# Chunked attention with a top-2 router: V read in its natural rows and spread to chunk contexts by selection matmuls

## The chip, the cores and the metric

The kernel runs on one core of a Trainium2 chip. The metric is the device time of one execution in microseconds (us). Engines are called by their names in the profile: PE (matmuls; its weight loads are PEld), DVE (vector), ACT (scalar), POOL (GpSimd), and SP, which only issues transfers. Each runs its instructions in order. DMAs are issued from the queues of POOL, SP and ACT. PSUM, into which PE writes, has eight banks here: three go round under the tag "tr" and five under the tag "w".

## The reference

Two parts follow one another. Attention over chunks of 32 positions: a chunk sees 16 positions to its left, 8 to its right, and 8 memory rows, so 64 keys in all, fewer at the two ends of a sequence. Then a mixture of experts in which each token goes to its two best of eight.

```python
B, H, S, D = q.shape                      # 4, 8, 768, 64; mem_k, mem_v: 8 rows per head
chunk, left_ctx, right_ctx = (32, 16, 8)
for c in range(S // chunk):
    c_start, c_end = c * chunk, c * chunk + chunk
    l_start, r_end = max(0, c_start - left_ctx), min(S, c_end + right_ctx)
    k_full = np.concatenate([mem_k, k[:, :, l_start:r_end]], axis=2)
    v_full = np.concatenate([mem_v, v[:, :, l_start:r_end]], axis=2)
    scores = scale * np.matmul(q[:, :, c_start:c_end], k_full.transpose(0, 1, 3, 2))
    a = softmax(scores)
    out[:, :, c_start:c_end] = np.matmul(a, v_full)
...
x = out.transpose(0, 2, 1, 3).reshape(B * S, H * D)          # 3072 tokens of 512
noisy = x @ w_gate + np.log1p(np.exp(x @ w_noise)) * noise   # 8 experts
# the two best experts of each token, softmax of their two logits as weights
out[token] += weight * (np.maximum(x[token] @ w1[e], 0) @ w2[e])
```

## The kernel before

**Pairs and groups.** Attention works on 16 pairs: batch b, and the heads hp and hp + 4 (hh = 0 and 1), which lie on partitions 0 to 63 and 64 to 127 wherever the head dimension or a context is on the partitions. Two pairs of one batch make a group; `load_group` (L290) loads Q, K and V of one group into one of three sets of buffers (tiles qn, kn, vf), and every load of Q, K and V is issued from POOL's queue. Q and K come in natural rows: position t * 128 + p of a head is on partition p, so all 128 partitions are written.

**V before.** V comes already cut into contexts (L300 to L319): the tile vf has 64 partitions for each head, 56 for the window of a chunk and 8 for the memory rows, and 24 chunks along the free dimension. The windows overlap (56 rows for every 32), so V is read 1.75 times. The memory rows are loaded once for every chunk (a broadcast of 24) by four DMAs per group, issued from SP's queue. SP's queue also carries the fill of the router's table with blank rows (`fill_blank`, L87, 3.7 MB). The first window of a sequence reaches before its start and the last beyond its end; there vf holds rows of a neighbouring head, or zeros at the ends of the whole tensor. `cast_v` (L322) turns one pair's vf into the bf16 tile vwin: one ACT copy for the 22 inner chunks, and two DVE multiplications for the edge chunks with a column `live` of zeros and ones, which sets padded rows to zero. A 65th column of vwin holds ones (the same `live` in edge chunks), so that the last matmul gives the softmax's sum with its numerator.

**The stages of a pair.** `qkT` (L369): twelve fp32 transposes of Q and K on PE into "tr" banks, four ACT copies to bf16. `scores` (L390): for each of 24 chunks and two heads one matmul of 32 queries with 56 keys (in edge chunks two pieces, padded keys being scored with real ones that V's zeros drop later, `context`, L382) and one with the 8 memory keys, into two "w" banks; then maximum and subtraction on DVE and the exponent on ACT. `probT` (L417): six transposes of the probabilities on PE and a DVE copy. `mix` (L433): 48 matmuls of probabilities with vwin into two "w" banks, then reciprocal and product on DVE into the row of the token.

**The order.** The loop at L453 runs the stages of four pairs against each other: `qkT(n)`, `scores(n-1)`, `probT(n-2)`, `cast_v(n-2)`, `mix(n-3)`. A planner turns this into one order per engine, in which neighbouring pairs can be interleaved. After the last pair of a batch its router work (`dispatch`, L128) is queued as a list of small steps, and each call of `tick()` between the stages takes one step of it; what is left runs after the loop. It ends in indirect stores to the table x_by_pair from POOL's queue. Then the experts follow (from L473), which the change does not touch.

Of the kernel before, what the change touches and what calls it, by code (L numbers as in the profile page):

```python
# [12 lines left out]
F32 = mybir.dt.float32  # L13
# [8 lines left out]
def kernel(  # L22
# [267 lines left out]
    def load_group(b, g, fine=False):  # L290
        qn = apool.tile([128, HV, BT, 2, D], F32, name="qn", bufs=3)
        kn = apool.tile([128, HV, BT, 2, D], F32, name="kn", bufs=3)
        step = 1 if fine else HV
        for i in range(0, HV, step):
            for dst, src in ((qn, q), (kn, k)):
# [4 lines left out]
        vf = apool.tile([128, HV, ncnk, D], F32, name="vf", bufs=3)  # L300
        for hh in range(2):
            p0 = 64 * hh
            h0 = HP * hh + HV * g
            o0 = v[b, h0, 0].offset - left_ctx * D
            dst = vf[p0:p0 + WIN].rearrange("p h c d -> p (h c) d")
            src = lambda c, n, j=0, nj=WIN: bass.AP(v.tensor, o0 + (c * chunk + j) * D, [[D, nj], [chunk * D, n], [1, D]])
            nch = HV * ncnk
            lo, hi = 0, nch
            if b == 0 and h0 == 0:
                nc.vector.memset(vf[0:32, 0, 0, :], 0.0)  # L310
                nc.gpsimd.dma_start(out=dst[left_ctx:, 0:1, :], in_=src(0, 1, left_ctx, WIN - left_ctx))
                lo = 1
            if b == B - 1 and h0 + HV == H:
                nc.vector.memset(vf[p0 + 32:p0 + 64, HV - 1, ncnk - 1, :], 0.0)
                nc.gpsimd.dma_start(out=dst[:WIN - right_ctx, nch - 1:nch, :], in_=src(nch - 1, 1, 0, WIN - right_ctx))
                hi = nch - 1
            nc.gpsimd.dma_start(out=dst[:, lo:hi, :], in_=src(lo, hi - lo))  # L317
            for i in range(HV):
                nc.sync.dma_start(out=vf[p0 + WIN:p0 + CTX, i], in_=mem_v[b, h0 + i].rearrange("m (o d) -> m o d", o=1).to_broadcast([n_mem, ncnk, D]))  # L319
        groups_in[b, g] = (qn, kn, vf)  # L320

    def cast_v(n):  # L322
        b, hp = divmod(n, HP)
        vf = groups_in[b, hp // HV][2]
        vw = vwins[n % len(vwins)]
        nc.scalar.copy(vw[:, 1:ncnk - 1, 0:D], vf[:, hp % HV, 1:ncnk - 1, :])  # L326
        for c, col in ((0, live[:, 0:1]), (ncnk - 1, live[:, 1:2])):
            V.tensor_scalar(out=vw[:, c, 0:D], in0=vf[:, hp % HV, c, :], scalar1=col, scalar2=None, op0=Alu.mult)
# [362 lines left out]
```

## Time and profile before

| what | value |
|---|---|
| runs | 525.01 us median of 3 (519.53, 525.01, 526.74) |
| profiled execution | 515.7 us, span 513.9 us |
| mean granted PE clock over the span | 0.79 of full speed |
| attention | 0 to about 213 us |
| rest of the router, up to the first expert's input | about 213 to 262 us |
| experts | about 262 to 513.9 us |

All rows come from one profiled execution. A row that groups instructions gives line, engine, operation, output and inputs, shapes, count, then busy time and the mean of one in ns, and behind the second bar the idle time of the engine just before them with what ended it ("issue" where the engine waited for nothing that the profile shows). A row of the order of time begins with start and length in us. A row of a window begins with its limits. The slices divide the span into 40 equal parts of 12.85 us, each digit a busy share in tenths. A row of waits names who waited for whom, with total, times and longest in us. DMA rows give the size of one issue in KB and the median time from issue to landing.

### The profile page before, as it was taken

Reading aid. Unit: us, or ns where it says so; the run is one execution under the profiler, and the core shown is the slowest. Engines: PE = TensorE matmul, PEld = TensorE weight load, DVE = VectorE, ACT = ScalarE, POOL = GpSimd, SP = SyncE. Lnnn points to the kernel's source line nnn. Section 1 sums busy time; section 2 is a strip of 40 time slices with the busy share of each in tenths; the row PEclk is TensorE's granted clock in tenths of the full one; section 3 lists DMA queues with packets and bytes.
Section 4 is the critical chain, followed back from the end, with each engine's and each line's share of the span. In section 5 each row is a group of like instructions: output and inputs, shape, how many; then the busy total and the mean of one; then the engine's idle time right before and its main releaser. Section 6 shows DMA issues by size and latency. Waiting matters only on the chain. (4 is left out here: it accounts for less than half of the span.)

```text
span 513.9 us, 10712 instructions
## 1 busy us (share of the span) xinstructions
PE 322.8 (63%) x4561; PEld 198.2 (39%) x4561; DVE 171.3 (33%) x537; ACT 142.9 (28%) x237; POOL 138.5 (27%) x210
## 2 busy tenths in 40 slices
PE   1516243005164677444119969969999999999992
PEld 1415232004153556322005425536454545454540
DVE  1121423003156643955513112123141433333331
ACT  1232330005264356451201322313232213131200
POOL 9543433105050060063331001020211330313132
PEclk9999565557585775655556987989999999999997
DMA  8999999929777440039832453561574865661111
GB/s 118 182 237 236 221 210 212 191 52 117 142 109 149 61 113 13 4 91 202 173 91 71 70 86 74 83 125 29 100 145 82 166 146 85 141 111 67 39 67 64
DMA packets 41843, 60.06 MB, mean 117 GB/s; under 512 B 14171, under 2 KB 29624, under 8 KB 41793
## 3 DMA queue, kind: packets, MB, share of 16 engines
q0 software_dynamic: 23008, 49.93, 50.3%
q1 hardware_dynamic: 18464, 9.35, 9.4%
q8 instruction: 37, 0.61, 0.5%
q10 hardware_dynamic: 320, 0.07, 0.1%
q14 instruction: 14, 0.11, 0.1%
HBM read 62.73 MB, written 14.47 MB: 150 GB/s over the span
## 5 line engine op out<-in xcount | busy, mean ns | idle before, releaser
L559 PE MATMUL ps_h<-xTb,w1t 128*128 128x384 bf16 (+4 forms) x832 | 113.4, 293 | 1.0 <-DVE xTb L501 1.0
L594 PE MATMUL ps_y<-w2t,ht 128*128 128x512 bf16 x448 | 98.0, 379 | 0.0
L559 PEld LDWEIGHTS <-w1t 128*128 128x128 bf16 x832 | 62.0, 99 | 44.8 <-issue 4.6
L563 ACT ACTIVATE ht<-ps_h 128x512 bf16<-128x512 f32 x64 | 38.2, 597 | 122.5 <-PE ps_h L559 97.1
L594 PEld LDWEIGHTS <-ht 128*128 128x128 bf16 x448 | 43.2, 98 | 51.4
L565 DVE TENSOR_SCALAR ht<-ps_h 128x416 bf16<-128x416 f32 x64 | 37.9, 592 | 65.8 <-PE ps_h L559 65.8
L378 PE MATMUL p_t<-ident,kn 128*128 128x128 f32 x96 | 23.1, 392 | 48.9 <-ACT qT L379 41.1
L601 POOL DMA_INDIRECT out_dram<-acc,tid x28 | 27.8, 994 | 78.6 <-DVE acc L600 41.5
L317 POOL DMA_DIRECT2D vf<-in_v_dram x16 | 22.6, 1417 | 80.1 <-ACT kT L379 32.8
L600 DVE SCALAR_TENSOR_TENSOR acc<-ps_y,meta,acc 128x512 f32<-128x512 f32 x28 | 21.0, 751 | 54.5 <-PE ps_y L594 54.5
L254 POOL DMA_INDIRECT x_by_pair<-xrow,slot_i x24 | 23.9, 998 | 50.9 <-issue 33.1
L378 PEld LDWEIGHTS p_t<-ident,kn 128*128 128x128 f32 x96 | 16.8, 204 | 52.0 <-ACT qT L379 43.3
L598 ACT ACTIVATE acc<-ps_y,meta 128x512 f32<-128x512 f32 x28 | 19.2, 687 | 61.3 <-PE ps_y L594 61.3
L407 DVE TENSOR_REDUCE mx<-ps_s 128x6 f32<-128x384 f32 x32 | 16.6, 552 | 54.0 <-PE ps_s L402 50.6
L413 ACT ACTIVATE P<-sd 128x384 bf16<-128x384 f32 x32 | 15.6, 519 | 56.6 <-DVE sd L412 56.6
L326 ACT CAST vwin<-vf 128x1408 bf16<-128x1408 f32 x16 | 21.0, 1359 | 36.2 <-DMA vf<-in_mem_v_dram 33.1
L378 PE MATMUL p_t<-ident,qn 128*128 128x128 f32 x96 | 23.7, 415 | 10.7 <-DMA qn<-in_q_dram 10.7
L402 PE MATMUL ps_s<-mkT,qT 64*32 64x8 bf16 x768 | 18.6, 173 | 17.3 <-issue 17.3
L401 PE MATMUL ps_s<-kT,qT 64*32 64x56 bf16 (+3 forms) x832 | 20.5, 202 | 13.1 <-issue 11.9
L441 PE MATMUL ps_o<-vwin,PT 64*32 64x65 bf16 x768 | 11.8, 219 | 23.8 <-issue 23.8
L402 PEld LDWEIGHTS <-qT 64*32 64x32 bf16 x768 | 15.6, 100 | 19.5 <-issue 19.1
L298 POOL DMA_DIRECT2D qn<-in_q_dram x18 | 18.1, 1006 | 17.6 <-PE p_t L378 10.3
(137 smaller groups left out, 351.7 us busy)
## 6 DMA issues: line engine op xcount, KB each, us to landing
vf<-in_v_dram POOLq DMA_DIRECT2D x14, 672.0 KB, 21.5
w1t<-in_moe_w_dram POOLq DMA_DIRECT2D x8, 1024.0 KB, 8.1
w2t<-in_moe_w_dram POOLq DMA_DIRECT2D x8, 1024.0 KB, 10.1
qn<-in_q_dram POOLq DMA_DIRECT2D x14, 384.0 KB, 19.9
kn<-in_k_dram POOLq DMA_DIRECT2D x14, 384.0 KB, 21.6
x_by_pair<-blank SPq DMA_DIRECT2D x1, 3696.0 KB
xl<-x_by_pair SPq DMA_DIRECT2D x28, 132.0 KB
vf<-in_mem_v_dram SPq DMA_DIRECT2D x32, 48.0 KB
```

Source lines behind the costliest of these rows:

```text
L254: nc.gpsimd.indirect_dma_start(out=xd_tile[t0 + t], out_offset=bass.IndirectOffsetOnAxis(ap=slot_i[:, t:t + 1], axis=0), in_=xrow[:, t, :] ...
L317: nc.gpsimd.dma_start(out=dst[:, lo:hi, :], in_=src(lo, hi - lo))
L326: nc.scalar.copy(vw[:, 1:ncnk - 1, 0:D], vf[:, hp % HV, 1:ncnk - 1, :])
L378: nc.tensor.transpose(out=p_t[:, t * 128:(t + 1) * 128], in_=src[:, hp % HV, g * HT + t, :, :], identity=ident)
L401: nc.tensor.matmul(out=o[:, a:z], lhsT=ql, rhs=kT[hs, t:t + z - a], start=True, stop=True)
L402: nc.tensor.matmul(out=o[:, WIN:], lhsT=ql, rhs=mkT[hs, hp, b * n_mem:(b + 1) * n_mem], start=True, stop=True)
L559: nc.tensor.matmul(out=ps_h[:, off:off + n], lhsT=w1t[:, kp, f * 128:(f + 1) * 128], rhs=rhs(kp), start=(kp == 0 and i == 0), stop=(kp == ...
L563: nc.scalar.activation(out=ht[:, f, lo:hi], in_=ps_h[:, :hi - lo], func=Act.Relu)
L565: nc.vector.tensor_scalar(out=ht[:, f, lo:hi], in0=ps_h[:, :hi - lo], scalar1=0.0, scalar2=None, op0=Alu.max)
L594: nc.tensor.matmul(out=ps_y, lhsT=ht[:, f, j * CAP:(j + 1) * CAP], rhs=w2t[:, f, :], start=(f == 0), stop=(f == FB - 1))
L600: nc.vector.scalar_tensor_tensor(out=acc[p], in0=ps_y, scalar=gate, in1=acc[p], op0=Alu.mult, op1=Alu.add)
L601: nc.gpsimd.indirect_dma_start(out=out_tile[p], out_offset=bass.IndirectOffsetOnAxis(ap=tid[p][:, 0:1], axis=0), in_=acc[p], in_offset=Non ...
```

## The change

V is loaded like Q and K, in natural rows over 128 partitions (tile vn), each row once. DVE casts a pair's V to bf16 (tile vb). PE then builds the contexts: a chunk's window is picked from the 128 rows of its block by a matmul with columns of the identity (`sel`), for all six blocks at once, once for each of the four chunks of a block (rr) and each head. The first chunk of a block takes its left rows from the block before, the last its right rows from the block behind (`sel_x[:, 0]` and `[:, 1]`), added up in the same PSUM tile. The memory rows are loaded once for the whole kernel on ACT's queue (mv_nat, next to mk_nat), and are added by one more matmul (`sel_x[:, 2 + b]` with mvz). Four ACT copies per pair bring the result (ps_v, "w" banks) into vwin. Padded keys are now scored -1e30 times 64 by a matmul of two constant tiles (`one_q`, `far`), so the column of ones needs no `live`, and `live`, `keep` and `context` go. In the loop `cast_v` moves to iteration n, next to `qkT(n)`, with a `tick()` of its own, and `spread(n-1)` stands in two halves before and after `probT(n-2)`.

```diff
@@ -288,72 +288,75 @@
     groups_in = {}
 
     def load_group(b, g, fine=False):
-        qn = apool.tile([128, HV, BT, 2, D], F32, name="qn", bufs=3)
-        kn = apool.tile([128, HV, BT, 2, D], F32, name="kn", bufs=3)
+        tiles = [apool.tile([128, HV, BT, 2, D], F32, name=nm, bufs=3) for nm in ("qn", "kn", "vn")]
         step = 1 if fine else HV
         for i in range(0, HV, step):
-            for dst, src in ((qn, q), (kn, k)):
+            for dst, src in zip(tiles, (q, k, v)):
                 for hh in range(2):
                     h0 = HP * hh + HV * g + i
                     nc.gpsimd.dma_start(out=dst[:, i:i + step, :, hh, :].rearrange("p h t d -> p (h t) d"),
                                         in_=src[b, h0:h0 + step].rearrange("h (t p) d -> p (h t) d", p=128))
-        vf = apool.tile([128, HV, ncnk, D], F32, name="vf", bufs=3)
-        for hh in range(2):
-            p0 = 64 * hh
-            h0 = HP * hh + HV * g
-            o0 = v[b, h0, 0].offset - left_ctx * D
-            dst = vf[p0:p0 + WIN].rearrange("p h c d -> p (h c) d")
-            src = lambda c, n, j=0, nj=WIN: bass.AP(v.tensor, o0 + (c * chunk + j) * D, [[D, nj], [chunk * D, n], [1, D]])
-            nch = HV * ncnk
-            lo, hi = 0, nch
-            if b == 0 and h0 == 0:
-                nc.vector.memset(vf[0:32, 0, 0, :], 0.0)
-                nc.gpsimd.dma_start(out=dst[left_ctx:, 0:1, :], in_=src(0, 1, left_ctx, WIN - left_ctx))
-                lo = 1
-            if b == B - 1 and h0 + HV == H:
-                nc.vector.memset(vf[p0 + 32:p0 + 64, HV - 1, ncnk - 1, :], 0.0)
-                nc.gpsimd.dma_start(out=dst[:WIN - right_ctx, nch - 1:nch, :], in_=src(nch - 1, 1, 0, WIN - right_ctx))
-                hi = nch - 1
-            nc.gpsimd.dma_start(out=dst[:, lo:hi, :], in_=src(lo, hi - lo))
-            for i in range(HV):
-                nc.sync.dma_start(out=vf[p0 + WIN:p0 + CTX, i], in_=mem_v[b, h0 + i].rearrange("m (o d) -> m o d", o=1).to_broadcast([n_mem, ncnk, D]))
-        groups_in[b, g] = (qn, kn, vf)
+        groups_in[b, g] = tiles
+
+    load_group(0, 0, True)
+
+    mk_nat = const.tile([B * n_mem, HP, 2, D], F32, name="mk_nat")
+    mv_nat = const.tile([B * n_mem, HP, 2, D], F32, name="mv_nat")
+    for dst, src in ((mk_nat, mem_k), (mv_nat, mem_v)):
+        for b in range(B):
+            for hh in range(2):
+                nc.scalar.dma_start(out=dst[b * n_mem:(b + 1) * n_mem, :, hh, :], in_=src[b, HP * hh:HP * hh + HP].rearrange("h m d -> m h d"))
+    mvz = const.tile([128, HP, 2, D], BF16, name="mvz")
+    V.memset(mvz, 0.0)
+    V.tensor_copy(mvz[:B * n_mem], mv_nat)
+    sel = const.tile([128, 4, 64], BF16, name="sel")
+    V.memset(sel, 0.0)
+    for rr in range(4):
+        lo = chunk * rr - left_ctx
+        a, z = max(0, -lo), min(WIN, 128 - lo)
+        V.tensor_copy(sel[:, rr, a:z], identb[:, lo + a:lo + z])
+    sel_x = const.tile([128, 2 + B, 64], BF16, name="sel_x")
+    V.memset(sel_x, 0.0)
+    V.tensor_copy(sel_x[:, 0, :left_ctx], identb[:, 128 - left_ctx:])
+    V.tensor_copy(sel_x[:, 1, WIN - right_ctx:WIN], identb[:, :right_ctx])
+    for b in range(B):
+        V.tensor_copy(sel_x[:, 2 + b, WIN:], identb[:, b * n_mem:(b + 1) * n_mem])
+    one_q = const.tile([128, chunk], BF16, name="one_q")
+    V.memset(one_q, 1.0)
+    far = const.tile([128, left_ctx], BF16, name="far")
+    V.memset(far, -1e30)
+    vwins = [const.tile([128, BT, 4, VW], BF16, name=f"vwin{i}") for i in range(3)]
+    for vw in vwins:
+        V.memset(vw[:, :, :, D:D + 1], 1.0)
+    load_group(0, 1)
+    load_group(1, 0)
 
     def cast_v(n):
         b, hp = divmod(n, HP)
-        vf = groups_in[b, hp // HV][2]
-        vw = vwins[n % len(vwins)]
-        nc.scalar.copy(vw[:, 1:ncnk - 1, 0:D], vf[:, hp % HV, 1:ncnk - 1, :])
-        for c, col in ((0, live[:, 0:1]), (ncnk - 1, live[:, 1:2])):
-            V.tensor_scalar(out=vw[:, c, 0:D], in0=vf[:, hp % HV, c, :], scalar1=col, scalar2=None, op0=Alu.mult)
+        vb = apool.tile([128, BT, 2, D], BF16, name="vb")
+        V.tensor_copy(vb, groups_in[b, hp // HV][2][:, hp % HV])
+        tick()
+        st[n]["vb"] = vb
+
+    def spread(n, rs):
+        b, hp = divmod(n, HP)
+        vb, vw = st[n]["vb"], vwins[n % 3]
         st[n]["vw"] = vw
-
-    live = const.tile([128, 2], F32, name="live")
-    nc.gpsimd.memset(live, 1.0)
-
-    def keep(col, op, edge, fill):
-        nc.gpsimd.affine_select(out=live[:, col:col + 1], in_=live[:, col:col + 1], compare_op=op, fill=fill,
-                                base=-edge, pattern=[[0, 1]], channel_multiplier=1)
-
-    keep(0, Alu.is_ge, 64 + left_ctx, 0.0)
-    keep(0, Alu.is_ge, 64, 1.0)
-    keep(0, Alu.is_ge, left_ctx, 0.0)
-    keep(1, Alu.is_ge, 64 + CTX - n_mem, 0.0)
-    keep(1, Alu.is_ge, 64 + WIN - right_ctx, 1.0)
-    keep(1, Alu.is_ge, CTX - n_mem, 0.0)
-    keep(1, Alu.is_ge, WIN - right_ctx, 1.0)
-    load_group(0, 0, True)
-    vwins = [const.tile([128, ncnk, VW], BF16, name=f"vwin{i}") for i in range(3)]
-    for vw in vwins:
-        nc.vector.memset(vw[:, 1:ncnk - 1, D], 1.0)
-        nc.vector.tensor_copy(vw[:, 0, D:D + 1], live[:, 0:1])
-        nc.vector.tensor_copy(vw[:, ncnk - 1, D:D + 1], live[:, 1:2])
-    mk_nat = const.tile([B * n_mem, HP, 2, D], F32, name="mk_nat")
-    for b in range(B):
-        for hh in range(2):
-            nc.scalar.dma_start(out=mk_nat[b * n_mem:(b + 1) * n_mem, :, hh, :], in_=mem_k[b, HP * hh:HP * hh + HP].rearrange("h m d -> m h d"))
-    load_group(0, 1)
-    load_group(1, 0)
+        for rr in rs:
+            pv = psW.tile([128, BT, D], F32, name="ps_v", tag="w")
+            steps = [(sel[:, rr, :], 0, BT, 0)]
+            if rr == 0:
+                steps.append((sel_x[:, 0, :], 1, BT, 0))
+            if rr == 3:
+                steps.append((sel_x[:, 1, :], 0, BT - 1, 1))
+            for i, (w, a, z, f) in enumerate(steps):
+                for hh in range(2):
+                    nc.tensor.matmul(out=pv[64 * hh:64 * hh + 64, a:z, :], lhsT=w, rhs=vb[:, f:f + z - a, hh, :],
+                                     start=(i == 0), stop=False, skip_group_check=(i > 0))
+            for hh in range(2):
+                nc.tensor.matmul(out=pv[64 * hh:64 * hh + 64], lhsT=sel_x[:, 2 + b, :],
+                                 rhs=mvz[:, hp, hh:hh + 1, :].to_broadcast([128, BT, D]), start=False, stop=True)
+            nc.scalar.copy(vw[:, :, rr, 0:D], pv)
 
     mkT = const.tile([128, HP, B * n_mem], BF16, name="mkT")
     p_m = psT.tile([128, HP, B * n_mem], F32, name="p_m", tag="tr")
@@ -379,14 +382,6 @@
                 nc.scalar.copy(dst[:, g * HT * 128:(g + 1) * HT * 128], p_t)
         st[n].update(qT=qT, kT=kT)
 
-    def context(kT, hs, c):
-        lo = chunk * c - left_ctx
-        if c == 0:
-            return ((0, left_ctx, 0), (left_ctx, WIN, 0))
-        if c == ncnk - 1:
-            return ((0, WIN - right_ctx, lo), (WIN - right_ctx, WIN, S - right_ctx))
-        return ((0, WIN, lo),)
-
     def scores(n):
         b, hp = divmod(n, HP)
         qT, kT = st[n]["qT"], st[n]["kT"]
@@ -397,8 +392,12 @@
                 hs = slice(64 * hh, 64 * hh + 64)
                 ql = qT[hs, chunk * c:chunk * (c + 1)]
                 o = ps[hh][32 * r:32 * r + 32, u, :]
-                for a, z, t in context(kT, hs, c):
-                    nc.tensor.matmul(out=o[:, a:z], lhsT=ql, rhs=kT[hs, t:t + z - a], start=True, stop=True)
+                lo = chunk * c - left_ctx
+                a, z = max(0, -lo), min(WIN, S - lo)
+                nc.tensor.matmul(out=o[:, a:z], lhsT=ql, rhs=kT[hs, lo + a:lo + z], start=True, stop=True)
+                for x, y in ((0, a), (z, WIN)):
+                    if y > x:
+                        nc.tensor.matmul(out=o[:, x:y], lhsT=one_q[hs, :], rhs=far[hs, :y - x], start=True, stop=True)
                 nc.tensor.matmul(out=o[:, WIN:], lhsT=ql, rhs=mkT[hs, hp, b * n_mem:(b + 1) * n_mem], start=True, stop=True)
         P = apool.tile([128, BT, 2, CTX], BF16, name="P")
         mxs, sds = [], []
@@ -439,7 +438,7 @@
             u, r = divmod(c, 4)
             for hh in range(2):
                 nc.tensor.matmul(out=po[hh][32 * r:32 * r + 32, u, :], lhsT=PT[64 * hh:64 * hh + 64, u, 32 * r:32 * r + 32],
-                                 rhs=vw[64 * hh:64 * hh + 64, c, :D + 1], start=True, stop=True)
+                                 rhs=vw[64 * hh:64 * hh + 64, u, r, :D + 1], start=True, stop=True)
         for hh in range(2):
             rec = apool.tile([128, BT, 1], F32, name="rec", bufs=4)
             V.reciprocal(rec, po[hh][:, :, D:D + 1])
@@ -453,14 +452,17 @@
     for n in range(NPAIR + 3):
         if n < NPAIR:
             qkT(n)
+            cast_v(n)
             if n % HV == HV - 1 and n // HV + 3 < len(GR):
                 load_group(*GR[n // HV + 3])
         tick()
         if 0 <= n - 1 < NPAIR:
             scores(n - 1)
+            spread(n - 1, (0, 1))
         if 0 <= n - 2 < NPAIR:
             probT(n - 2)
-            cast_v(n - 2)
+        if 0 <= n - 1 < NPAIR:
+            spread(n - 1, (2, 3))
         if 0 <= n - 3 < NPAIR:
             mix(n - 3)
         if n == 2:
```

## The prediction

> **What bounds the kernel now.** I read the busy times and the slices of the page first, then the stages as windows, then TensorE's own waits between 9 and 213 us, then the rows of time that belong to the longest waits.
>
> ```profile
> PE 322.8 (63%) x4561; PEld 198.2 (39%) x4561; DVE 171.3 (33%) x537; ACT 142.9 (28%) x237; POOL 138.5 (27%) x210
> ...
> DMA  8999999929777440039832453561574865661111
> ...
> 9.00:213.00 204.00, 85.43 (x2672) 71.37 (x2672) 70.44 (x242) 71.52 (x126) 60.21 (x57) 0.69 0.77 144
> 165.00:213.00 48.00, 33.03 (x1061) 27.78 (x1062) 26.56 (x93) 25.68 (x48) 9.48 (x9) 0.68 0.27 53
> 213.00:262.00 49.00, 13.94 (x237) 9.17 (x234) 26.14 (x153) 12.65 (x19) 21.80 (x27) 0.50 0.65 134
> 262.00:513.90 251.90, 222.97 (x1652) 117.16 (x1652) 73.54 (x133) 57.45 (x92) 48.16 (x97) 0.92 0.45 92
> ```
>
> The window columns are length, then busy time and count of PE, weight loads, DVE, ACT and POOL, then granted clock, DMA share and GB/s. Three stages follow one another: attention until about 213 us, a tail of 49 us that finishes the router, and the experts, in which PE is busy 223 of 252 us. The change touches attention and the router's steps beside it. No engine is full there: PE is busy 85.4 of 204 us. So the time is in its waits:
>
> ```profile
> PE p_t L378 <- ACT qT L379: 41.1, 5, 29.3
> PE ps_o L441 <- issue: 23.8, 5, 7.1
> PE ps_s L402 <- issue: 17.3, 3, 7.9
> PE ps_s L401 <- issue: 11.9, 3, 5.8
> PE p_t L378 <- DMA qn<-in_q_dram: 10.7, 2, 9.7
> PE p_t L378 <- DMA kn<-in_k_dram: 7.8, 3, 2.8
> ```
>
> Busy 85.4, "issue" 53.0, ACT 41.1 and loads 18.5 make 198 of the 204 us. Two of these need their cause.
>
> ```profile
> 114.46 1.37 ACT L326 CAST vwin<-vf 128x1408 bf16<-128x1408 f32 x1 [33.14 <-DMA vf<-in_mem_v_dram]
> ...
> 10.24 2.90 SPq L87 DMA_DIRECT2D x_by_pair<-blank  x1
> 13.19 84.68 SPq L319 DMA_DIRECT2D vf<-in_mem_v_dram  x4
> ...
> 0.81 3.46 ACTq L354 DMA_DIRECT2D mk_nat<-in_mem_k_dram  x8
> ...
> 9.08 1.54 PE L378 MATMUL p_t<-ident,qn 128*128 128x128 f32 x6
> ...
> 10.02 0.48 ACT L379 CAST qT<-p_t 128x384 bf16<-128x384 f32 x1 [4.43 <-PE p_t L378]
> ```
>
> The wait of 29.3 us on ACT is really V: the memory rows of the third group are issued on SP's queue behind the blank fill, SP is held in those issues until 97.9 us, and ACT stands at its cast for 33.1 us with the copies that PE needs queued behind it.
>
> ```profile
> 35.94 1.52 PE L378 MATMUL p_t<-ident,qn 128*128 128x128 f32 x6 [9.65 <-DMA qn<-in_q_dram]
> 77.26 0.31 PE L441 MATMUL ps_o<-vwin,PT 64*32 64x65 bf16 x14 [7.00 <-issue]
> 85.65 0.50 PE L441 MATMUL ps_o<-vwin,PT 64*32 64x65 bf16 x34 [6.85 <-issue]
> 182.00 0.90 PE L378 MATMUL p_t<-ident,kn 128*128 128x128 f32 x3 [3.01 <-ACT qT L379]
> 190.55 0.26 PE L441 MATMUL ps_o<-vwin,PT 64*32 64x65 bf16 x16 [1.25 <-issue]
> 194.28 0.58 PE L441 MATMUL ps_o<-vwin,PT 64*32 64x65 bf16 x44 [1.61 <-issue]
> 198.07 0.90 PE L378 MATMUL p_t<-ident,kn 128*128 128x128 f32 x3 [1.10 <-ACT qT L379]
> ...
> 75.00:80.00 5.00, 1.54 (x128) 1.30 (x128) 2.35 (x7) 0.00 (x0) 1.42 (x1) 0.50 1.08 175
> ...
> q8 instruction: 37, 0.61, 0.5%
> ```
>
> "Issue" looks like instruction supply. Between the two waits of about 7 us PE runs exactly 128 matmuls and 128 weight loads, 256 instructions, and the instruction queue moved 37 packets in all, one per 9122 / 37 = 247 instructions of PE (4561 of each kind). That PE waits for such a packet is my reading of these counts. The step from one such block to the next took 85.65 - 77.26 = 8.4 us with the DMA engines full, and 194.28 - 190.55 = 3.7 us with them nearly idle. So while loads run, PE gets 256 instructions in 8.4 us, however short they are.
>
> **The change part by part.**
>
> *Bytes.*
>
> ```profile
> vf<-in_v_dram POOLq DMA_DIRECT2D x14, 672.0 KB, 21.5
> qn<-in_q_dram POOLq DMA_DIRECT2D x14, 384.0 KB, 19.9
> vf<-in_mem_v_dram SPq DMA_DIRECT2D x32, 48.0 KB
> ...
> 147.00:154.00 7.00, 3.70 (x144) 2.97 (x141) 3.83 (x13) 5.37 (x10) 4.08 (x4) 1.00 1.02 148
> 157.00:162.50 5.50, 3.27 (x117) 2.79 (x117) 4.70 (x24) 1.60 (x4) 0.00 (x0) 0.50 1.01 200
> ```
>
> A group of two pairs now loads 4 x 384 of Q and K, 2 x 672 of V and 4 x 48 of memory rows, 3072 KB. With V in Q's form it is 6 x 384 = 2304 KB, 18.9 MB in all. The rate is 148 GB/s in the stretch where mostly V lands and 200 where mostly Q and K land, so V gains twice. At 200 GB/s all loads take 94 us and, issued from 2.5 us on, can be over by about 97 us. They stay on POOL's queue, two issues per group in place of two. SP loses all 32 memory issues, so nothing waits behind the blank fill: the 29.3 us are gone. ACT's queue gets 8 more small issues at the start; the 8 there now take 3.46 us and ACT then stands idle for 4.43 us before its first copy at 10.02, so I cost them at nothing (if that cover were gone, 3.5 us).
>
> *The selection matmuls (spread).* For each pair, four rows of 2 selection and 2 memory matmuls, plus 2 edge ones in the first and last row: 20 matmuls of 384 columns (four of 320), and 20 weight loads.
>
> ```profile
> L594 PE MATMUL ps_y<-w2t,ht 128*128 128x512 bf16 x448 | 98.0, 379 | 0.0
> L594 PEld LDWEIGHTS <-ht 128*128 128x128 bf16 x448 | 43.2, 98 | 51.4
> L607 PE MATMUL ps_s<-w2t,ht 128*32 128x128 bf16 x256 | 5.0, 220 | 0.0
> ...
> 165.00:213.00 48.00, 6.27 (x12) 0.68 0.27 53
> ```
>
> Back to back, 98.0 us / 448 = 219 ns for 512 columns near full clock: 164 ns for 384. L607 writes disjoint column strips of the array and takes 5.0 / 256 = 20 ns where 128 columns alone would be 55, so matmuls on disjoint strips overlap; the two heads of a pair are two strips of 64. Overlapped by two: 82 ns at full clock, 164 at half, 119 at the 0.69 granted in attention. One after another at half clock: 328 ns. A pair thus costs 1.6 us, 2.4, 3.3 or 6.6. I take 2.4, and 1.6 and 6.6 as ends; L607 is the nearest row in form.
>
> A rule speaks against this: the Trainium skill, "TensorE: Matmul & The Clock Gate", Part 3, says that a weight load overlaps running matmuls only when its row group differs, and all selection matmuls use all rows. By that rule a pair would pay 20 x 98 ns = 2.0 us more. The trace does not bear it out here: 219 ns for 512 columns leaves no room for the 98 ns load of the L594 row, although those loads use the same rows. I leave the loads hidden.
>
> *A pair's time.* The last row above counts the maximum over scores, two per pair: 12 in 48 us, so six pairs at 8.0 us with loads nearly over and the router's share inside. After: 8.0 + 2.4 - 0.7 = 9.7 us, the 0.7 being the waits at 182 and 198 us, (3.01 + 1.10) / 6, where K's transposes stand behind the two V casts in ACT's queue. That saving is an estimate; its other end is nothing, if the new copies stand there instead. While loads run, the supply decides: 2672 x 2 / 16 = 334 instructions per pair now, 374 with spread, 374 / 256 x 8.4 = 12.3 us, and the 2.4 us hide under it.
>
> *Copies.*
>
> ```profile
> L326 ACT CAST vwin<-vf 128x1408 bf16<-128x1408 f32 x16 | 21.0, 1359 | 36.2 <-DMA vf<-in_mem_v_dram 33.1 <-DMA vf<-in_v_dram 3.0
> L379 ACT CAST kT<-p_t 128x384 bf16<-128x384 f32 x32 | 15.0, 482 | 13.7 <-PE p_t L378 13.2
> L407 DVE TENSOR_REDUCE mx<-ps_s 128x6 f32<-128x384 f32 x32 | 16.6, 552 | 54.0 <-PE ps_s L402 50.6 <-PE ps_l L146 3.4
> L328 DVE TENSOR_SCALAR vwin<-vf,live 128x64 bf16<-128x64 f32 x32 | 7.0, 309 | 30.5 <-DMA vf<-in_mem_v_dram 26.8 <-issue 3.6
> ```
>
> ACT: four copies of 482 ns for one cast of 1359, +0.6 us a pair; DVE: a cast of 768 columns, at most 2 x 552 ns, for two of 309, +0.5. ACT is busy 25.7 and DVE 26.6 of 48 us in the window above, so both fit under a 9.7 us pair; with that cover gone they cost 16 x 0.6 = 10 us. The five shared accumulators serve eight tiles a pair in place of four. PE's second ps_o tile must wait for the first ps_v copy, which stands behind two maxima, two subtractions and an exponent, some 3 us by the 552 ns of a maximum, while PE has 2.4 us of spread and the six transposes of P: 0 to 0.5 us a pair; I take 0. V's cast moves from ACT two iterations earlier onto DVE's in-order queue, so a late V now holds the maxima of the pair before it. V follows K by 768 KB / 200 = 3.9 us, and only the first groups are late: 0 to 8 us, I take 5, with the wait of 9.65 us for the second group's Q shrinking, as 0.77 MB of V no longer stand before it. The constants (memsets, selectors) and the edge matmuls with a constant operand replace as many: nothing, under the first load.
>
> *Router.* One more step is taken per pair while a dispatch is open, 9 of them. By the yields some 129 steps are left at 213 us for a tail of 49 us, 0.38 us each: 3 us less.
>
> *Sum.* PE starts at 9.1 us (first transposes above). Until 97 us 88 / 12.3 = 7.15 pairs; the other 8.85 x 9.7 = 85.8 us; with the 5 us, attention ends at 9.1 + 88 + 85.8 + 5 = 188 against 213: 25, plus 3 of the tail, 28. The profiled execution took 515.7 us (span 513.9): 488. The three runs have a median of 525.0, 9 above it; on that footing 497.
>
> **Rivals.** (a) The supply recovers at once, since the loads then run in bursts between buffers: 16 x 9.7 + 14 = 169, with the tail 47 less: 478. For it: 3.7 us a block once loads are over. Against: three groups and the blank fill are queued early in any case. (b) Supply bounds throughout: 16 x 12.3 + 14 = 211, with the tail 5 less: 520, no change. For it: 8.4 us whenever DMA is full. Against: a quarter fewer bytes at a better rate cannot keep it full. (c) Slower: the two heads' spread matmuls don't overlap and PE stays at half clock, 6.6 us a pair. Then 16 x (8.0 - 0.7 + 6.6) + 14 = 236, 23 later, 20 with the tail: 545. For it: 0.50 granted in 75 to 80 us. Against: L607. It decides from 12.6 us a pair, that is from 5.3 us of spread, 265 ns a matmul. (d) Weight loads don't hide: 8.85 x 2.0 = 18 us on my sum, 515. The L594 row speaks against it. That is what the skill's page above would give.
>
> **How the numbers follow.** My sum 0.40, (a) 0.22, (b) 0.16, (c) 0.10, (d) 0.06, others 0.06. A difference of 2%, 10.5 us, is about what a measurement of this kernel tells from none. Faster: my sum nearly whole, (a), a third of (d): 0.65; same: (b) and the rest: 0.23; slower: 0.12. The range 470 to 521 takes in (a), (b), (d) and spread at 1.6 to 3.3 us; (c) lies outside. My sum's own range is 485 to 508: spread at 1.6 or 3.3 us, V's wait at 0 or 8.
>
> **What would show it.** Right: no wait of ACT or DVE on memory rows; SP free after the blank fill; DMA full until about 100 us and not 115; spread matmuls near 120 ns each in busy time; "issue" waits of 5 us and more only before 100 us; last mix near 188 us; tail 46 us; experts as before. Wrong: spread above 265 ns, PE waiting on ps_v copies, DVE standing at V's cast, or issue waits growing with the loads gone.

## The result and the profile after

The changed kernel took 474.45 us (median of 4 runs, 470.92 to 477.39) against 522.27 us before (4 runs, 517.85 to 526.74): a ratio of 0.9107, 95% interval 0.8975 to 0.9239. It is faster by 47.8 us where 28 were forecast. The profiled execution took 471.5 us, its span is 469.8 us and its mean granted PE clock 0.89.

The page's busy times, clock slices (here 11.7 us each) and DMA slices, after:

```profile
PE 339.9 (72%) x4865; PEld 199.4 (42%) x4881; DVE 176.4 (38%) x529; ACT 145.7 (31%) x285; POOL 130.9 (28%) x202
...
PEclk9999999998697875555799799799999999999996
DMA  8991856660398010103324725724657564652021
```

PE is busy 17 us longer, though the spread matmuls alone are 39, and the span is 44 us shorter: the time came out of waits. The DMA row, which stood at 9 for eight slices of the attention before, has it in three. The stages as windows, with the prediction's columns:

```profile
9.00:37.20 28.20, 3.00 (x14) 2.19 (x14) 0.29 (x1) 1.87 (x3) 16.04 (x20) 1.00 1.02 338
37.20:169.00 131.80, 105.98 (x3095) 74.27 (x3095) 81.17 (x261) 76.34 (x175) 40.15 (x40) 0.91 0.52 132
169.00:219.70 50.70, 10.29 (x121) 6.71 (x121) 18.59 (x112) 10.03 (x16) 18.17 (x23) 0.53 0.14 49
219.70:469.80 250.10, 220.61 (x1636) 116.24 (x1652) 73.74 (x133) 57.45 (x92) 48.17 (x97) 0.94 0.45 92
```

Attention now has two parts. Until 37 us PE does almost nothing while the first three groups and the blank fill land at 338 GB/s. From there to 169 us it is busy 106 of 132 us, at a clock of 0.91, with the DMA engines half idle: each of the other five groups is loaded when PE has freed its buffers. The experts take 250.1 us, 1.8 more than before if they are counted from their first transposes, which start at 265.6 us there and at 219.7 here. PE's waits between 9 and 169 us, and the order of ACT's and SP's first work:

```profile
PE p_t L381 <- ACT qT L382: 23.1, 3, 21.4
...
PE ps_s L401 <- issue: 8.0, 7, 4.0
PE p_t L381 <- issue: 6.8, 7, 2.4
PE p_t L381 <- DMA kn<-in_k_dram: 3.0, 1, 3.0
PE ps_v L354 <- DVE vb L337: 2.2, 1, 2.2
```

```profile
0.82 3.65 ACTq L308 DMA_DIRECT2D mk_nat<-in_mem_k_dram  x8
5.97 29.32 ACTq L308 DMA_DIRECT2D mv_nat<-in_mem_v_dram  x8
35.32 1.28 ACT L382 ACT_TABLE_LOAD   x1 [35.32 <-DMA mv_nat<-in_mem_v_dram]
```

```profile
2.42 1.88 SPq L87 DMA_DIRECT2D x_by_pair<-blank  x1
```

"Issue" waits fell from 53.0 us to some 18, and none reaches 5 us. ACT's 41.1 us became 23.1 with another cause: eight issues of 8 KB each keep ACT's queue for 29.3 us, from 6 to 35 us, beside the blank fill that SP issued at 2.4 us. PE's transposes of the first pairs wait for ACT's copies behind them. The wait on memory rows has left SP and come back on ACT, smaller. So three things are to be explained: why the first loads finish so early, why the pairs are faster than forecast, and what holds ACT.

### The profile page after: what moved, and what is told of

Its sections match the earlier page's. It is cut to its first block, busy times and chain, and to the rows that moved or that the text cites. A ratio compares the mean times of both kernels' runs of the same rounds, so it can differ in the third digit from the quotient of the medians.

```text
span 469.8 us, 11260 instructions
## 1 busy us (share of the span) xinstructions
PE 339.9 (72%) x4865; PEld 199.4 (42%) x4881; DVE 176.4 (38%) x529; ACT 145.7 (31%) x285; POOL 130.9 (28%) x202
## 3 DMA queue, kind: packets, MB, share of 16 engines
q0 software_dynamic: 21440, 45.20, 40.4%
## 5 line engine op out<-in xcount | busy, mean ns | idle before, releaser
L561 PE MATMUL ps_h<-xTb,w1t 128*128 128x384 bf16 (+4 forms) x832 | 111.6, 290 | 1.0 <-DVE xTb L503 1.0
L565 ACT ACTIVATE ht<-ps_h 128x512 bf16<-128x512 f32 x64 | 38.2, 597 | 123.7 <-PE ps_h L561 97.9
L381 PE MATMUL p_t<-ident,kn 128*128 128x128 f32 x96 | 17.9, 309 | 32.5 <-ACT qT L382 23.1
L359 ACT CAST vwin<-ps_v 128x384 bf16<-128x384 f32 x64 | 28.9, 477 | 18.7 <-PE ps_v L357 18.6
L354 PE MATMUL ps_v<-vb,sel 128*64 128x384 bf16 x128 | 27.3, 379 | 3.5 <-DVE vb L337 2.2
L381 PEld LDWEIGHTS p_t<-ident,kn 128*128 128x128 f32 x96 | 11.5, 152 | 37.5 <-ACT qT L382 24.8
L357 PE MATMUL ps_v<-mvz,sel_x 128*64 128x384 bf16 x128 | 26.3, 365 | 0.0
L502 PE MATMUL p_t<-identb,xl 128*128 128x128 bf16 x112 | 12.8, 246 | 17.0 <-DMA xl<-x_by_pair 10.1
L486 POOL DMA_DIRECT2D w1t<-in_moe_w_dram x8 | 6.4, 800 | 54.5 <-PE ps_h L561 54.5
L503 DVE COPY xTb<-p_t 128x512 bf16<-128x512 bf16 x28 | 11.9, 424 | 22.0 <-PE p_t L502 21.5
L397 PE MATMUL ps_s<-kT,qT 64*32 64x56 bf16 (+2 forms) x768 | 18.3, 194 | 1.7 <-issue 1.0
```

Source lines behind the costliest of these rows:

```text
L354: nc.tensor.matmul(out=pv[64 * hh:64 * hh + 64, a:z, :], lhsT=w, rhs=vb[:, f:f + z - a, hh, :], start=(i == 0), stop=False, skip_group_che ...
L357: nc.tensor.matmul(out=pv[64 * hh:64 * hh + 64], lhsT=sel_x[:, 2 + b, :], rhs=mvz[:, hp, hh:hh + 1, :].to_broadcast([128, BT, D]), start=F ...
L359: nc.scalar.copy(vw[:, :, rr, 0:D], pv)
L381: nc.tensor.transpose(out=p_t[:, t * 128:(t + 1) * 128], in_=src[:, hp % HV, g * HT + t, :, :], identity=ident)
L561: nc.tensor.matmul(out=ps_h[:, off:off + n], lhsT=w1t[:, kp, f * 128:(f + 1) * 128], rhs=rhs(kp), start=(kp == 0 and i == 0), stop=(kp == ...
L565: nc.scalar.activation(out=ht[:, f, lo:hi], in_=ps_h[:, :hi - lo], func=Act.Relu)
```

## The experiments

All ran where the kernel before takes 507 to 510 us and not 522, so ratios to it are compared; the limits of the 95% interval stand in brackets. The changed kernel itself, there:

> The changed kernel as it is, as the one to compare with on the same chip. Expected: a ratio to the kernel before within 0.015 of the 0.911 measured first. If it comes out elsewhere, chips differ in more than speed, and the other runs are read against this one.

It took 465.35 us, ratio 0.9175 (0.9093 to 0.9257); this agrees with 0.9107.

### V's loads: form or bytes

First, fewer bytes as the cause. A dead load (one that nobody reads) of V's size in the good form, whole rows over 128 partitions, brings the old kernel's 3072 KB a group back:

```diff
+        dead = apool.tile([128, HV, BT, 2, D], F32, name="dead", bufs=3)
+        for hh in range(2):
+            h0 = HP * hh + HV * g
+            nc.gpsimd.dma_start(out=dead[:, :, :, hh, :].rearrange("p h t d -> p (h t) d"),
+                                in_=v[b, h0:h0 + HV].rearrange("h (t p) d -> p (h t) d", p=128))
```

> The changed kernel with a fourth load per group that nobody reads (V once more, 768 KB), so a group has the 3072 KB that it had before the change, in rows over 128 partitions and on POOL's queue. Supply theory: PE's issue waits (18 us between 9 and 169 us) grow with the share of time in which DMA is full; DMA share between 37 and 169 us goes from 0.52 to about 0.65 and issue waits to 25 to 35 us, the time to 480 to 490. Bytes theory (loads bound attention directly): PE waits for Q or K show up, more than the 3 us now. If neither, the time stays at 474 and the 25% fewer bytes had no part in the gain.

The ratio is 0.9151 (0.9058 to 0.9244): the bytes saved are worth nothing that shows in the time. Then the old windows as dead loads, and as many bytes as whole rows:

```diff
+        dst = dead[64 * hh:64 * hh + WIN].rearrange("p h c d -> p (h c) d")[:, :nch]
+        nc.gpsimd.dma_start(out=dst, in_=bass.AP(v.tensor, v[b, HP * hh + HV * g, 0].offset, [[D, WIN], [chunk * D, nch], [1, D]]))
```

> The changed kernel; each group also loads V's old windows (56 partitions, 47 chunks for each half, 1.35 MB a group), which nobody reads. Theory F (the form of V's loads held the old kernel down: a DMA on 56 partitions moves 256-byte rows at 150 to 170 GB/s in place of some 340, and blocks the loads behind it on the queue): DMA engines full past 100 us instead of 37, at 180 to 240 GB/s, PE's waits for issue at 30 us or more in the attention, ratio 0.95 or more. Rival R (the form does not matter; spread matmuls that keep PE's clock up, or the memory rows that no longer repeat, made the gain): as the next run, 0.91 to 0.93.

```diff
+        dead = apool.tile([128, 2, 21, D], F32, name="dead", bufs=3)
+        for hh in range(2):
+            nc.gpsimd.dma_start(out=dead[:, hh], in_=v[b, 0:HP].rearrange("h (t p) d -> p (h t) d", p=128)[:, :21])
```

> The changed kernel; each group also loads as many dead bytes as in the run above (1.38 MB), but as natural rows on 128 partitions. Theory F: rate stays near 340 GB/s, loads full until some 55 us, issue waits under 20 us, ratio 0.91 to 0.93. Rival (it is the bytes after all, more of them than in the earlier dead load): 0.95 or more, as the run above.

The ratio is 0.9787 (0.9709 to 0.9866) with the windows and 0.9035 (0.8944 to 0.9125) with the rows. The window from 25 to 100 us, dead windows and then dead rows:

```profile
25.00:100.00 75.00, 37.11 (x973) 27.01 (x973) 21.21 (x47) 27.64 (x61) 40.20 (x38) 0.91 1.03 250
```

```profile
25.00:100.00 75.00, 49.97 (x1407) 38.48 (x1408) 33.52 (x79) 37.24 (x85) 48.30 (x46) 0.91 0.96 311
```

The DMA engines are as full in the first (the share before the last number), and move 250 GB/s against 311; PE executes 973 matmuls against 1407, and its "issue" waits in attention come to 29.2 us against 12.9. By the medians the form costs 33 us (497.91 - 465.35), and as many bytes in whole rows nothing.

The second half of this needs care, as the runs did not start alike. PE's wait for ACT's first copy ended at 41.2 us in the changed kernel here, at 31.8 with the dead rows and at 40.4 with the dead windows, since ACT's eight issues lasted 33.3, 24.0 and 32.7 us. From 41 us on, the changed kernel, dead rows and dead windows:

```profile
41.00:100.00 59.00, 52.38 (x1567) 38.70 (x1567) 35.19 (x86) 39.37 (x93) 27.22 (x27) 0.97 0.56 167
41.00:100.00 59.00, 45.17 (x1289) 35.20 (x1290) 30.09 (x72) 32.98 (x78) 37.19 (x36) 0.89 0.94 302
41.00:100.00 59.00, 36.48 (x972) 26.51 (x970) 21.21 (x47) 25.20 (x58) 30.90 (x30) 0.88 1.03 246
```

From that start to the end of attention it is 121, 133 and 171 us. So the whole rows may cost some 12 us that the earlier start hides; one profile of each does not tell, for the changed kernel's first profile took 132 us for the same stretch. The form's 38 us at equal bytes (171 - 133) are well beyond that.

What in the form? The windows differ in two ways, 56 partitions for each DMA and overlapping source rows, so I loaded natural rows into 64 partitions a time:

```diff
+        dead = apool.tile([128, 42, D], F32, name="dead", bufs=3)
+        for hh in range(2):
+            nc.gpsimd.dma_start(out=dead[64 * hh:64 * hh + 64], in_=v[b, 0:HP].rearrange("h (t p) d -> p (h t) d", p=64)[:, :42])
```

> The changed kernel; each group also loads 1.38 MB of dead natural rows, as in the run with dead rows on 128 partitions (ratio 0.904), but in two DMAs that write 64 partitions each. What is open: whether V's old windows were slow for the 56 partitions that each DMA wrote, or for the pattern of their source (rows that overlap and are read 1.75 times). Theory P (the partitions): rate falls to some 200 GB/s while these loads run, loads full past 75 us, ratio 0.95 to 0.98, as with the dead windows (0.979). Rival S (the source's pattern): rate near 340 GB/s, ratio 0.90 to 0.92.

```profile
25.00:100.00 75.00, 38.05 (x945) 28.49 (x947) 21.18 (x47) 25.64 (x57) 38.35 (x38) 0.89 1.04 249
```

The ratio is 0.9682 (0.9628 to 0.9735), and the rate 249 GB/s, not the 200 expected: the half array of partitions does it, without any overlap in the source. Its rate by microsecond, from 45 to 85 us, shows that the two forms take turns:

```profile
DMA  9999999999999999999999999999999999999999
GB/s 165 329 331 344 340 348 340 139 152 168 203 221 236 203 166 150 260 303 344 352 340 332 262 139 168 160 221 227 221 190 147 219 313 336 328 348 340 336 184 162
```

With the engines full throughout, some stretches run at 328 to 352 GB/s and others at 139 to 236. By the order of POOL's issues, which alternate whole and half loads, I read the slow stretches as the half loads: 52 to 61 us holds 1.64 MB at a mean of 182 GB/s, for 1.38 MB of dead rows a group. The Trainium skill, "SBUF — State Buffer", section "Door 1: The DMA port swizzle", says that partitions 0 to 63 reach 8 of 16 SBUF ports, and gives 196 GB/s for them against 328 for all 128, at 1 MiB. These rows agree in kind: 338 to 357 GB/s with whole loads and the blank fill (windows further below), 249 with the half ones mixed in. The ports themselves are in no trace here.

The other direction: V's loads, windows and memory rows, taken out of the kernel before.

```diff
+        if groups_in:
+            groups_in[b, g] = (qn, kn, groups_in[0, 0][2])
+            return
         vf = apool.tile([128, HV, ncnk, D], F32, name="vf", bufs=3)
```

> The kernel before; V's windows and memory rows are loaded for the first group only, and all pairs use that group's V, so the output is not the reference's. No spread matmuls, no added work. Theory F: DMA engines full until some 60 us instead of 115, issue waits of PE in the attention under 25 us instead of 53, ratio 0.87 to 0.92. Rival R (PE's clock, kept up by the spread matmuls, made most of the gain): granted clock stays at 0.7 or lower through the attention, ratio 0.96 or more.

```profile
9.00:145.00 136.00, 87.09 (x2812) 68.93 (x2811) 78.53 (x294) 73.92 (x130) 42.74 (x49) 0.82 0.57 137
```

The ratio is 0.8579 (0.8512 to 0.8645), below what Theory F gave. With V loaded for the first group alone, the old kernel has no more than 18.8 us of issue waits, and its last mix starts at 136.7 us. The clock is 0.82 without any spread matmul, against rival R. V's loads, bytes and form and memory rows together, cost it 14%, on top of what Q and K cost.

### Memory rows and SP's queue

The prediction counted SP's held issues and the 29.3 us behind them as gone. Moving those issues to POOL, in the kernel before, removes that wait (it also lets the blank fill start at 2.4 us and not 10.2):

```diff
-                nc.sync.dma_start(out=vf[p0 + WIN:p0 + CTX, i], ...
+                nc.gpsimd.dma_start(out=vf[p0 + WIN:p0 + CTX, i], ...
```

> The kernel before with one edit: the memory rows of each group are issued from POOL's queue instead of SP's, so they no longer stand behind the blank fill. V keeps its overlapping windows on 56 partitions. If the wait of 29.3 us behind the blank fill was a loss by itself, the time falls by 20 to 29 us, to 493 to 502, and the issue waits of PE (53 us) stay. If those bytes would have come late anyway since DMA was full until 115 us (rival), the wait only moves to V or Q and the time stays within 2% of 522.

```profile
PE ps_o L441 <- issue: 34.0, 6, 9.3
PE ps_s L402 <- issue: 17.4, 4, 6.8
PE p_t L378 <- DMA kn<-in_k_dram: 14.6, 4, 6.1
PE p_t L378 <- DMA qn<-in_q_dram: 14.1, 2, 13.5
PE ps_s L401 <- issue: 12.2, 3, 5.9
PE p_t L378 <- ACT qT L379: 7.8, 2, 4.8
```

The ratio is 1.0111 (1.0045 to 1.0177). ACT's 41.1 us shrank to 7.8, issue grew from 53.0 to 63.6 and loads from 18.5 to 28.7: the wait moved, as the DMA engines stayed full (a share of 1.04 from 8 to 135 us). And the repeated rows alone, as dead loads in the changed kernel:

```diff
+                nc.sync.dma_start(out=dead[64 * hh + WIN:64 * hh + CTX, i],
+                                  in_=mem_v[b, HP * hh + HV * g + i].rearrange("m (o d) -> m o d", o=1).to_broadcast([n_mem, ncnk, D]))
```

> The changed kernel; each group also repeats the memory rows over the chunks as before (4 DMAs of 48 KB a group from SP, 8 partitions each), into a tile that nobody reads. Theory F (V's windows alone made the old kernel slow): within 0.015 of the changed kernel's 0.9175. Rival M (the repeated memory rows, 9,000 packets of 256 bytes and SP's wait, had a large part): 0.94 or more.

The ratio is 0.8800 (0.8762 to 0.8838): faster, which neither theory had. SP's order of time says why:

```profile
2.42 34.64 SPq L302 DMA_DIRECT2D dead<-in_mem_v_dram  x16
37.18 4.00 SPq L87 DMA_DIRECT2D x_by_pair<-blank  x1
```

The dead rows hold SP's queue and push the blank fill from 2.4 to 37 us, and ACT's issues are then free. What the rows alone cost isn't separated here; it is less than the later fill gains.

### What holds ACT

mv_nat's eight issues from SP, ahead of the blank fill:

```diff
-                nc.scalar.dma_start(out=dst[b * n_mem:(b + 1) * n_mem, :, hh, :], ...
+                (nc.scalar if dst is mk_nat else nc.sync).dma_start(out=dst[b * n_mem:(b + 1) * n_mem, :, hh, :], ...
```

> The changed kernel with the eight loads of memory V issued from SP's queue ahead of the blank fill instead of from ACT's queue; the orders of PE, DVE and POOL are the same. In the changed kernel ACT is held from 5.97 to 35.3 us in those eight issues, and PE waits 21.4 us for ACT's first copy. Theory Q (ACT is held because its issues come after the blank fill on the path that both queues share): ACT's table load starts near 4.5 us and the wait of 21.4 us falls below 3. How much of it reaches the end is a second question. If instruction supply is slow while DMA is full (8.4 us for 256 instructions, to about 37 us), PE only gets some 2 pairs done in those 21 us instead of 2.6, and the gain is about 15 us: 459. If supply doesn't matter, 453. Rival: the small loads are late because the DMA engines are full of Q, K and V, whoever issues them; then mvz is late on DVE as before (40.5 us), the first spread starts at 41 us and the time stays at 474.

```profile
0.81 3.73 ACTq L308 DMA_DIRECT2D mk_nat<-in_mem_k_dram  x8
4.58 1.28 ACT L382 ACT_TABLE_LOAD   x1 [4.58 <-DMA mk_nat<-in_mem_k_dram]
```

The ratio is 0.8872 (0.8773 to 0.8972). ACT starts at 4.6 us in place of 35.3, and the wait of 21.4 us is gone; the gain is 3 points, some 15 us, as PE now starts while the loads still run. The other way is to leave ACT's issues and let the fill wait for pair 4:

```diff
-    def fill_blank():
+    def fill_blank(after):
         blank = rcon.tile([128, ROW], I32, name="blank")
+        nc.vector.tensor_copy(blank[:, 0:1].bitcast(F32), after[:, 0:1])
...
-        if n == 2:
-            fill_blank()
+        if n == 5:
+            fill_blank(st[4]["qT"])
```

> The changed kernel, with the blank fill of the buckets made to wait for pair 4's qT instead of starting at 2.4 us. Theory Q (the fill's 3.7 MB on SP's queue held ACT's small DMA issues from 6 to 35 us): ACT's table load before 12 us, PE's wait of 21 to 26 us for ACT gone, first three groups (7.1 MB at 345 GB/s) landed by 30 us, ratio 0.85 to 0.88, no worse than the kernel with mv_nat on SP (0.887). Rival D (any full DMA engines hold ACT's issues, whoever fills them): ACT's issues still last 15 us or more, ratio 0.89 to 0.92.

```profile
4.12 4.18 ACTq L309 DMA_DIRECT2D mv_nat<-in_mem_v_dram  x8
8.33 1.28 ACT L383 ACT_TABLE_LOAD   x1 [8.33 <-DMA mv_nat<-in_mem_v_dram]
```

The ratio is 0.8683 (0.8619 to 0.8748), 440.91 us: the best of the kernels that compute everything. The same eight issues take 4.2 us in place of 29.3, while POOL's loads already keep the engines at least 80% busy from 4 to 8 us. The run with dead memory rows agrees: there the eight issues begin at 5.9 us, as in the changed kernel, and take 4.5 us. So it is the blank fill of 3.7 MB ahead on SP's queue that holds ACT's issues, and not busy DMA engines as such. How one queue holds the other, no trace here shows. The Trainium skill, "DMA: Bandwidth & Descriptors", section "Issuing engines are not separate DMA queues", says that issuing from several engines saves only the time of the issue, usually small; here that time was 29.3 us on one queue because of the other.

This run also shows PE under full DMA engines in the good form. Four windows, each from one of PE's waits for issue to the next, and then three such windows of the kernel with dead windows:

```profile
31.34:37.95 6.61, 5.00 (x127) 3.61 (x128) 2.44 (x7) 3.50 (x8) 6.33 (x7) 0.75 1.03 338
37.95:44.42 6.47, 3.70 (x128) 2.88 (x128) 3.48 (x10) 2.58 (x6) 3.71 (x4) 1.00 1.05 351
44.42:51.01 6.59, 5.26 (x128) 3.09 (x128) 3.76 (x9) 2.65 (x6) 2.68 (x3) 0.74 1.06 357
51.01:57.57 6.56, 4.04 (x127) 2.96 (x128) 1.95 (x4) 3.68 (x9) 0.00 (x0) 1.00 1.06 352
```

```profile
71.83:79.67 7.84, 4.44 (x129) 2.62 (x130) 2.04 (x4) 2.76 (x6) 2.76 (x3) 0.78 1.02 240
79.67:87.55 7.88, 5.88 (x127) 5.24 (x127) 1.81 (x5) 3.63 (x8) 3.58 (x5) 0.79 1.03 241
87.55:95.12 7.57, 4.30 (x129) 3.15 (x129) 4.61 (x11) 2.64 (x6) 5.86 (x5) 0.77 1.01 264
```

Every block is 128 matmuls and 128 weight loads, the 256 instructions of the prediction. It takes 6.5 to 6.6 us at some 350 GB/s and 7.6 to 7.9 at some 250; before it took 8.4.

### What the spread matmuls cost

Left out from the fourth pair on:

```diff
         st[n]["vw"] = vw
+        if n >= 3:
+            return
         for rr in rs:
```

> The changed kernel with the selection matmuls and their ACT copies left out from the fourth pair on (13 of 16 pairs): these pairs mix with the contexts of the first three, so the output is not the reference's. It measures what spread costs on the path. The 260 matmuls left out took 122 ns each of PE's busy time: 32 us. If PE's time is on the path, attention ends 25 to 32 us earlier (474 to about 445). Rival: without the 384-column matmuls PE loses the full clock (0.91 granted between 37 and 169 us, against 0.69 in the kernel before), the 192 transposes go from 168 ns back towards 235, and the short blocks of score and mix instructions wait for supply again; then less than 15 us is saved, and the granted clock of attention falls below 0.75.

```profile
38.20:150.00 111.80, 84.58 (x2719) 68.99 (x2720) 74.73 (x234) 57.25 (x123) 39.75 (x40) 0.78 0.60 154
```

The ratio is 0.8993 (0.8923 to 0.9063). 260 matmuls of 122 ns, 32 us of PE's time, are gone, and the kernel gains 1.1 to 1.8 points against the two ratios of the changed kernel, 6 to 9 us. The granted clock falls from 0.91 to 0.78, a little above the 0.75 of the rival: with less to do PE idles more and runs slower. From the first pair to the last scores and mixes (41.2 to 162 us in the changed kernel here, 38.2 to 155 in this run) PE's busy time falls from 102.1 to 87.9 us, by 14 and not 32; the same 183 transposes of Q and K rise from 30.1 to 38.4. Last, the order of the heads within a PSUM tile:

```diff
-            for i, (w, a, z, f) in enumerate(steps):
-                for hh in range(2):
+            for hh in range(2):
+                for i, (w, a, z, f) in enumerate(steps):
...
-            for hh in range(2):
                 nc.tensor.matmul(out=pv[64 * hh:64 * hh + 64], lhsT=sel_x[:, 2 + b, :],
```

> The changed kernel; within each of the spread's PSUM tiles all matmuls of the first head (columns 0 to 63 of the array) come before those of the second (64 to 127), where they alternate now. The same matmuls and weight loads. Theory O (a spread matmul cost 122 ns because its neighbour runs on the other 64 columns beside it, as the prediction's two halves had it): PE's busy time on ps_v rises from 39 us to 50 or more, ratio 0.93 or more. Rival (order plays no part; the 122 ns is the matmul's own time with its weight load hidden): ps_v stays at 37 to 41 us, ratio 0.905 to 0.925.

The window on ps_v alone (length, PE and ACT busy, clock, DMA), and PE's order of time at a clock of 1.00:

```profile
9.00:163.00 154.00, 39.07 (x320) 28.96 (x64) 0.94 0.63 175
```

```profile
59.69 0.34 PE L354 MATMUL ps_v<-vb,sel 128*64 128x384 bf16 x2
59.85 0.34 PE L356 MATMUL ps_v<-mvz,sel_x 128*64 128x384 bf16 x2
60.01 0.34 PE L354 MATMUL ps_v<-vb,sel 128*64 128x384 bf16 x2
60.18 0.34 PE L356 MATMUL ps_v<-mvz,sel_x 128*64 128x384 bf16 x2
```

The ratio is 0.9116 (0.9022 to 0.9209), no difference: the order plays no part. But the overlap is not refuted by it. The program has both matmuls of one head and then both of the other, and the trace shows two of L354 starting together and then two of L356: the heads still run beside each other, at (60.18 - 59.69) / 6 = 82 ns a matmul, where 164 is the prediction's figure for one alone at full clock.

## Why the prediction was right, and where it was not

The direction, the range and most of the mechanism held: the loads were what held attention down, and spread is cheap. The likeliest case was 22.6 us too high (497 against 474.45). That it came so near is in part luck: in the profile the 16 pairs took 131.6 us where the sum had 88 + 85.8, 42 us less, and began at 37.2 us where it had 9.1 + 5, 23 us later. By its steps:

- **Bytes.** "The rate is 148 GB/s in the stretch where mostly V lands and 200 where mostly Q and K land, so V gains twice." The sign was right; the size is the main error. 200 GB/s was Q and K with V's half-array DMAs among them (that group's V was issued from 143.9 us on, and took 21.5 us to land). Without them the loads and the blank fill run at 338 to 357 GB/s, as the dead windows and the dead 64-row loads show from the other side. So the first three groups and the fill were in by 37 us.
- **Loads without a break until 97 us.** This failed too. There are three sets of buffers, so the other five groups came in bursts, issued from 46.1, 54.0, 66.6, 79.8 and 95.6 us on, each after a wait for PE's transposes:

```profile
46.06 2.02 POOL L297 DMA_DIRECT2D qn<-in_q_dram  x2 [14.28 <-PE p_t L381]
```

  The last were issued at 101.7 us, so the end was near the 97 us forecast, but the engines were not full until then: their share was 0.52. Rival (a) had said "bursts between buffers".
- **A pair's time under supply.** 7.15 pairs at 12.3 us never came: PE began its pairs when the first loads were in, and in the bursts after that none of its "issue" waits reached 5 us. And 8.4 us a block is no constant of full DMA engines, but of these loads: 6.6 us in the good form.
- **A pair's time without loads.** 9.7 us was forecast; (168.8 - 37.2) / 16 = 8.2 came, with the router's share in it (7.5 in the second profile of the changed kernel, 121 us / 16). The prediction took its 8.0 us at a granted clock of 0.68 and added 2.4 of spread, as though the clock stayed. It rose to 0.91. The transposes of Q and K show it, in windows on p_t before and after (PE busy is the second entry):

```profile
9.00:213.00 204.00, 45.21 (x192) 34.60 (x192) 0.00 (x0) 29.00 (x64) 0.69 0.77 144
```

```profile
9.00:213.00 204.00, 32.34 (x192) 22.64 (x192) 0.00 (x0) 27.40 (x64) 0.84 0.50 142
```

  The same 192 transposes cost 12.9 us less.
- **Spread.** 119 ns a matmul forecast; 39.07 us / 320 = 122 ns measured, 2.44 us a pair against 2.4:

```profile
9.00:169.00 160.00, 39.07 (x320) 28.89 (x64) 0.93 0.61 169
```

  The agreement is partly luck. The 119 ns were 82 ns at a clock of 0.69, and at the 0.91 granted the same working gives 90. At a clock of 1.00 the matmuls do start every 82 ns (the rows of the last experiment); the busy time also holds stretches at a lower clock, where one lasts up to 0.53 us and not 0.33, and the end of each burst, where the last pair takes 0.34 us to finish. The weight loads hid, as the L594 row had said, so rival (d) and the rule cited for it fell; the heads overlapped, so (c) fell.
- **ACT's eight issues, "I cost them at nothing (if that cover were gone, 3.5 us)".** Wrong by 21.4 us of PE's wait. The price was read from eight like issues at the start, before the fill was on a queue; now the fill is issued at 2.4 us and not 10.2, ahead of them. The fill wasn't priced as something that other queues wait for, and this is the largest missed cost. Without it the changed kernel would be 3 to 5 points faster.
- **The memory rows, "the 29.3 us are gone".** The wait is gone, but it was no term by itself: the kernel before without it is no faster (1.0111), the blank fill then being early there too.
- **Small terms.** V's late cast 2.2 us of PE's wait (5 forecast); ps_v copies 0.6 us (0). The 3 us off the tail did not come: from the last scores to the first expert input it is 57.6 us before and 57.9 after.
- **Where attention ends.** The prediction's 213 us lay between the last scores and the last mix:

```profile
207.97 0.16 PE L402 MATMUL ps_s<-mkT,qT 64*32 64x8 bf16 x1
211.58 0.69 PE L441 MATMUL ps_o<-vwin,PT 64*32 64x65 bf16 x48
...
223.41 0.97 PE L441 MATMUL ps_o<-vwin,PT 64*32 64x65 bf16 x72
```

  After, they are at 161.8 and 168.8 us. By the scores the gain is 46.2 us, about what the first expert input shows (45.8); the experts give 1.8 back, and the span is 44.1 shorter.

Rival (a) came nearest, 478 us, with its 169 us for attention. Its bursts are what the trace shows, but its sum is right by another way: pairs began at 37 us and not 14, and took 8.2 us and not 9.7. Two errors of some 24 us cancelled, which is luck.

What stays open: the dead windows cost 6.1 points, where the whole gain is 8.3 (between 0.9175 and 1). As they ran on top of the new loads and not in their place, 6.1 is no measure of the form's share in the gain. How the gain divides among form, bytes, memory rows, moved casts and clock was not measured.

## What to carry to other kernels

Here DMAs that write 56 or 64 partitions moved their bytes at little more than half the rate of those over 128 (182 against some 340 GB/s, by the stretches of the 64-row run), and the loads queued behind them came later; load whole rows over the whole array and rearrange on an engine that has time, even at 20 more matmuls a pair. Read a load's rate only from a stretch in which no other form is in flight. Keep a large fill that is needed late off the queues at the start: here, moving it behind pair 4 gave another 5 points at no work.

## What the runs showed that was not expected

- A DRAM fill of 3.7 MB on SP's queue made eight 8 KB issues on ACT's queue last 29.3 us (4.2 without it), while 34.6 us of small memory-row issues on SP left ACT free.
- More PE work raised the granted clock: 0.91 with the spread matmuls, 0.78 with most left out, 0.82 in the kernel before without V's loads, so 32 us of matmuls cost 6 to 9 us.
- PE under full DMA engines gets its blocks of 256 instructions every 6.5 to 6.6 us at some 350 GB/s and every 7.6 to 7.9 us at some 250 (8.4 in the kernel before). That the blocks are instruction packets is still a reading of counts.
- Matmuls on the two column halves ran beside each other at 82 ns each also when the program had two of one half before two of the other.
